# One gate over nine row tiles in place of two over four and five

## The chip, the core and the metric

The kernel runs on one core of one Trainium2 chip. The metric is the time on the device in microseconds (us), as the median of several executions; fewer is better. Six engines appear: TensorE (PE in the rows, with PEld for its weight loads), VectorE (DVE), ScalarE (ACT), GpSimd (POOL), SyncE (SP, which here only issues DMAs), and the DMA engines. Each of the first five works through its own queue of instructions strictly in order; an instruction whose input isn't there holds up everything behind it on that engine.

## The reference

Three stages follow one another on 2304 rows (4 sequences of 576) of 512 numbers.

```python
scores = scale * q @ k.T                       # 8 heads of 64, per sequence
thresh = max(scores) - tau
attn = softmax(where(scores >= thresh, scores, -1e9)) @ v      # x: 2304 x 512

noisy = x @ w_gate + log1p(exp(x @ w_noise)) * noise           # 8 experts
top2 = the two largest of noisy; weights = softmax over the two
out[row] = sum over its two experts of weight * relu(x @ w1[e]) @ w2[e]

# third stage: a skip score, the best of 8 experts, out = x + y for rows with a positive score
```

## The kernel before

**Attention.** Two heads are handled as a pair; four sequences of four pairs make 16 pairs (`PAIRS`). A pair is nine units of 128 rows of scores (`UNITS`), 144 in all. The loop over units (L770) is the schedule: it emits the scores of unit u+2 (`emit_S`, L291), the row maximum of u+1 (L299) and its exponential (L301), the transposes of the probabilities of u-1 (`emit_T`, L340, through one PSUM bank tagged `tp`) and the thresholded probabilities of u (L330). After a chunk of four or five units come products with v (`av`, L390 and L393) and the normalisation (`norm`, L400) into the transposed activations `xT`.

**Work in the background.** Between these steps the loop takes one step at a time from lists of generators: `bg` (gates), `bq` (first rows of expert 0), `fq` (fills and early weights), `pq` (scaling of k). `bg` is a queue: its second entry starts when the first has ended. A generator that yields 2 waits for a place where TensorE may be given work (`spare_pe`, L680, in six of the nine units of a pair); the others yield after about one VectorE instruction.

**The first gate.** `gate1(t0, n)` (L414) handles n row tiles of 128 rows: logits on TensorE in groups of up to four tiles (L157, transposed back at L162), some 45 small VectorE instructions on 128 x 8n elements, the rank of each row in its expert (`ranks`, L120: an array of n x 8 x n products and two matmuls, L135 and L136), the places of both choices (`ii`, L481), and then two scatters for each tile on POOL (L169) into the table `slots1`. Beside it `rows1` (L406) writes the n row tiles out to `x1` (L409 transposes, L411, L412). Logits, ranks, row transposes and the counts (`ct`, L630) all take the same PSUM bank as the transposes of the attention. `GATES` (L659) says at which pair and chunk the gates are put on `bg`: tiles 0 to 3 after pair 3, 4 to 8 after pair 7, 9 to 12 after pair 11; tiles 13 to 17 follow after the attention.

**The first experts.** Expert 0 starts on tiles 0 to 8 alone, expert 1 on tiles 0 to 12. `early_rows` (L711) is put on `bg` behind the second and the third gate. For expert 1 it loads `meta` from `slots1` by SP (L559), waits for all scatters so far, casts it to `tid` and `gid` on VectorE (L568, L570) and gathers rows of `x1` on POOL (L177). Then the layer of expert 0 begins: its weights are split in a high and a low part, `w1h` on ScalarE (L854) and `w1l` (L855) on POOL for the odd blocks and on VectorE for the even ones (L1135), and TensorE multiplies block by block (L612). The three first blocks are done earlier, in the last units (`early_mm1`).

Of the kernel before, what the change touches and what calls it, by code (L numbers as in the profile page):

```python
# [8 lines left out]
F32 = mybir.dt.float32  # L9
F32R = mybir.dt.float32r  # L10
I32 = mybir.dt.int32
# [11 lines left out]
E = 8  # L23
# [16 lines left out]
def attention_moe_moe(ctx, tc, qT, kT, vm, vr, tau, wgn, noise, w1a, w2a, wsg, w1b, w2b, out):  # L40
# [45 lines left out]
    wgn_t = const.tile([128, KD, 32], F32, name="wgn_t")  # L86
# [56 lines left out]
    def dot_e(pool, a, b, n, tag, r):  # L143
        w = pool.tile([128, n, E], F32, name="w" + tag)
        nc.vector.tensor_tensor(w, a, b, op=OP.mult)
        yield
        nc.vector.tensor_reduce(r[:, :, None], w, axis=AX.X, op=OP.add)
        yield

    def logits(pool, bank, parts, w, lz, i0):  # L150

        n = len(parts)
        yield 2
        ps = bank("lg")
# [48 lines left out]
    def pool(stack, name, bufs, side="left", **kw):  # L203
        return stack.enter_context(tc.tile_pool(name=name, bufs=bufs, side=side, reuse_waits="tile", **kw))
# [5 lines left out]
    g_p = pool(gctx, "g", 1)  # L210
# [7 lines left out]
    e_p = pool(actx, "e", 3, "right")  # L218
    pt_p = pool(actx, "pt", 2, "right")
    sm_p = pool(actx, "sm", 4, "right")  # L220
    ps_s = pool(actx, "ps_s", 3, space=PSUM)
    ps_x = pool(actx, "ps_x", 1, space=PSUM)
    ps_a = pool(actx, "ps_a", 1, space=PSUM)
# [9 lines left out]
    def xcols(t):  # L233
        return lambda kd: xTs[t * 128 // HN][:, kd, t * 128 % HN:t * 128 % HN + 128]
# [177 lines left out]
        nc.sync.dma_start(x1[t * 128:(t + 1) * 128, :], xr)  # L412

    def gate1(t0, n):  # L414
        sh = [128, n, E]
        lz = g_p.tile([128, n, 2 * E], F32, name="lz")
        for a in range(0, n, 4):
            yield from logits(g_p, bank, [xcols(t0 + i) for i in range(a, min(n, a + 4))], wgn_t, lz, a)
        z = lz[:, :, E:]
        u = g_p.tile(sh, F32, name="u")  # L420
        nc.vector.scalar_tensor_tensor(u, z, -1.0, z, op0=OP.mult, op1=OP.min)
        nc.scalar.activation(u, u, AF.Exp)
        yield from settle()
        w = g_p.tile(sh, F32, name="w")
        nc.vector.tensor_scalar(w, u, 2.0, None, op0=OP.add)
        yield
        nc.vector.reciprocal(w, w)
        yield
        nc.vector.tensor_tensor(w, w, u, op=OP.mult)
        yield  # L430
        nc.vector.tensor_tensor(u, w, w, op=OP.mult)
        yield
        ln = g_p.tile(sh, F32, name="ln")
        nc.vector.tensor_scalar(ln, u, 2.0 / 15, None, op0=OP.mult)
        yield
        for k in (13, 11, 9, 7, 5, 3):
            nc.vector.scalar_tensor_tensor(ln, ln, 2.0 / k, u, op0=OP.add, op1=OP.mult)
            yield
        nc.vector.scalar_tensor_tensor(ln, ln, 2.0, w, op0=OP.add, op1=OP.mult)
        yield  # L440
        nc.vector.scalar_tensor_tensor(ln, z, 0.0, ln, op0=OP.max, op1=OP.add)
        yield
        nz = g_p.tile(sh, F32, name="nz")
        nc.vector.tensor_tensor(nz, ln, noise_t[:, t0:t0 + n], op=OP.mult)
        yield
        nc.vector.tensor_tensor(nz, nz, lz[:, :, :E], op=OP.add)
        yield
        m1, o1 = yield from first_max(g_p, nz, n, "a")
        nc.vector.scalar_tensor_tensor(nz, o1, -3.0e38, nz, op0=OP.mult, op1=OP.add)
        yield  # L450
        m2, o2 = yield from first_max(g_p, nz, n, "b")
        mask = g_p.tile(sh, F32, name="mask")
        nc.vector.tensor_add(mask, o1, o2)
        d = g_p.tile([128, n], F32, name="d")
        nc.vector.tensor_sub(d, m2[:, :, 0], m1[:, :, 0])
        e2 = g_p.tile([128, n], F32, name="e2")
        nc.scalar.activation(e2, d, AF.Exp)
        yield
        rk = yield from ranks(g_p, bank, mask, run1, n)
        sl = g_p.tile(sh, F32, name="sl")  # L460
        nc.vector.tensor_tensor(sl, rk, ebase[:, None, :].to_broadcast(sh), op=OP.add)
        h7 = g_p.tile([128, n], F32, name="h7")
        nc.vector.tensor_scalar(h7, rk[:, :, E - 1], float(SL1), None, op0=OP.is_lt)
        yield
        dn = g_p.tile([128, n], F32, name="dn")
        nc.vector.tensor_scalar(dn, e2, 1.0, 1e-9, op0=OP.add, op1=OP.add)
        idx, meta = [], []
        for k in range(2):
            mt = g_p.tile([128, n, 2], F32, name=f"mt{k}")
            nc.vector.tensor_copy(mt[:, :, 0], tokid[:, t0:t0 + n])  # L470
            if k == 0:
                nc.vector.reciprocal(mt[:, :, 1], dn)
            else:
                nc.vector.tensor_tensor(mt[:, :, 1], e2, meta[0][:, :, 1], op=OP.mult)
            meta.append(mt)
            yield
        for k, o in enumerate((o1, o2)):
            ii = g_p.tile([128, n], I32, name=f"ii{k}")
            r = g_p.tile([128, n], F32, name=f"ir{k}")
            yield from dot_e(g_p, o, sl, n, "d", r)  # L480
            nc.vector.tensor_copy(ii, r)  # L481
            idx.append(ii)
            yield
        for i in range(n):
            for ii, mt in zip(idx, meta):
                scatter(slots1, ii[:, i:i + 1], mt[:, i], sc1)
                for _ in range(apart[0]):
                    yield 1
        nc.vector.tensor_tensor(h7, h7, mask[:, :, E - 1], op=OP.mult)
        nc.vector.tensor_scalar(not7[:, t0:t0 + n], h7, -1.0, 1.0, op0=OP.mult, op1=OP.add)  # L490
        yield
# [145 lines left out]
    bg = []  # L637
# [8 lines left out]
    def at(u, phase, f, *a):  # L646
        plan.setdefault((u, phase), []).append((f, a))
# [8 lines left out]
        return put  # L656

    WAITS = (4, 6)
    GATES = {(3, 1): (0, 4), (7, 1): (4, 5), (11, 1): (9, 4)}  # L659

    rq = []

# [107 lines left out]
    for u in range(NU):  # L770
        g, c, t, hh = UNITS[u]
        if (c, t, hh) == (0, 0, 0):
            if g + 1 < len(PAIRS):
                load_v(g + 1)
            if g == 12:
                early_pool()
                fq.append(early_raw())
                bq.append(early_xt())
            if g == len(PAIRS) - 1:
                pq.append(early_split())  # L780
        if (c, t, hh) == (0, 0, 0) and g + 2 < len(PAIRS):
            load_qk(g + 2)
        if (c, t, hh) == (1, 3, 0) and g + 2 < len(PAIRS):
            pq.append(prep(g + 2))
        if u + 2 < NU:
            emit_S(u + 2)
        else:
            early_mm1(u + 2 - NU)
        if u + 1 < NU:
            emit_max(u + 1)  # L790
        step(bg, 1, False)
        run(u, "mid")
        if u % 2 == 0:
            emit_th(u)
        step(bg, 1, False)
        step(bq, 1, False)
        if u:
            emit_T(u - 1)
        run(u, "pe")
        run(u, "end")  # L800
        emit_stt(u)
        step(pq)
        if u % 9 in (2, 3, 4, 6, 7, 8):
            spare_pe()
        else:
            step(bg, 1, False)
        if u % 4 == 3:
            step(fq)
        if (t, hh) == ((1, 1) if c == 0 else (4, 0)):
            k = (g, c)  # L810
            sums1(*k)
            at(u + 1, "mid", sums2, *k)
            at(u + 2, "pe", extra, *k)
            if c:
                at(u + 2, "pe", extra_mixed, g)
            for kt, (d, ph) in enumerate(AV[c]):
                at(u + d, ph, av, *k, kt)
            at(u + NORM[c][0], NORM[c][1], norm, *k)
            if k in GATES:
                at(u + 7, "end", bg.append, gate_and_rows(*GATES[k], True))  # L820
                if k[0] > 3:
                    at(u + 7, "end", bg.append, early_rows(*((e0a, 0) if k[0] == 7 else (e1a, 1))))
        if (c, t, hh) == (1, 2, 1):
            while pq:
                step(pq)
# [713 lines left out]
```

## Time and profile before

| | us |
|---|---|
| median of 3 runs | 1058.8 (1057.45 to 1059.7) |
| profiled execution | 1054.65 |
| its span, first to last instruction | 1052.9 |
| TensorE busy | 986.8 (94%) |
| VectorE busy | 586.3 (56%) |
| ScalarE busy | 495.0 (47%) |
| GpSimd busy | 305.9 (29%) |

The attention takes the first third: its last row maximum starts at 326.15. The rest is the two expert stages, in which TensorE is nearly always at work. Busy time of TensorE is that of matmuls which overlap, so 94% doesn't say that it could do no more. Where two engines hand work to and fro, the timeline shows who is late. "Clock" is the share of full speed that TensorE's clock was granted.

### The profile page before, as it was taken

Reading aid. Unit: us, or ns where it says so; the run is one execution under the profiler, and the core shown is the slowest. Engines: PE = TensorE matmul, PEld = TensorE weight load, DVE = VectorE, ACT = ScalarE, POOL = GpSimd, SP = SyncE. Lnnn points to the kernel's source line nnn. Section 1 sums busy time; section 2 is a strip of 40 time slices with the busy share of each in tenths; the row PEclk is TensorE's granted clock in tenths of the full one; section 3 lists DMA queues with packets and bytes.
Section 4 is the critical chain, followed back from the end, with each engine's and each line's share of the span. In section 5 each row is a group of like instructions: output and inputs, shape, how many; then the busy total and the mean of one; then the engine's idle time right before and its main releaser. Section 6 shows DMA issues by size and latency. Waiting matters only on the chain. (4 is left out here: it accounts for less than half of the span.)

```text
span 1052.9 us, 16933 instructions
## 1 busy us (share of the span) xinstructions
PE 986.8 (94%) x6262; PEld 776.4 (74%) x6262; DVE 586.3 (56%) x1480; ACT 495.0 (47%) x941; POOL 305.9 (29%) x417
## 2 busy tenths in 40 slices
PE   6999999999988898999999999999999987899995
PEld 3555555555545797889889998989898776799894
DVE  6887888787785762453333242423323365677463
ACT  4766766666665642343333333333333232555352
POOL 3121143126204542230313122121222366222210
PEclk9999999999999998999999999999999998899998
DMA  6434454145500654463535445252453730766550
GB/s 148 108 88 129 128 146 90 50 109 148 163 19 1 233 149 91 126 187 93 151 66 140 113 131 121 83 158 66 110 159 90 271 116 11 280 228 207 187 212 16
DMA packets 54856, 134.76 MB, mean 128 GB/s; under 512 B 20043, under 2 KB 26475, under 8 KB 46064
## 3 DMA queue, kind: packets, MB, share of 16 engines
q1 hardware_dynamic: 41344, 107.17, 32.7%
q0 software_dynamic: 13424, 26.45, 11.2%
q8 instruction: 51, 0.84, 0.4%
q14 instruction: 37, 0.30, 0.1%
HBM read 112.64 MB, written 23.69 MB: 129 GB/s over the span
## 5 line engine op out<-in xcount | busy, mean ns | idle before, releaser
L626 DVE SCALAR_TENSOR_TENSOR hl<-h,hh 128x128 fp32r<-128x128 f32 (+3 forms) x157 | 80.0, 510 | 166.3 <-ACT hh L625 147.1
L886 PE MATMUL y<-w2h,hh 128*128 128x512 f32 x418 | 170.4, 408 | 0.0
L886 PE MATMUL y<-w2h,hl 128*128 128x512 f32 x418 | 164.1, 393 | 0.0
L886 PE MATMUL y<-w2l,hh 128*128 128x512 f32 x418 | 163.4, 391 | 0.0
L625 ACT ACTIVATE hh<-h 128x128 fp32r<-128x128 f32 (+3 forms) x157 | 71.5, 455 | 193.5 <-PE h L612 147.4
L612 PE MATMUL h<-xh,w1h 128*128 128x320 f32 (+2 forms) x596 | 153.7, 310 | 2.7 <-ACT xh L594 1.4
L612 PE MATMUL h<-xh,w1l 128*128 128x320 f32 (+2 forms) x596 | 151.3, 306 | 2.1 <-POOL w1l L855 2.1
L612 PE MATMUL h<-xl,w1h 128*128 128x320 f32 (+2 forms) x596 | 151.9, 307 | 1.3 <-DVE xl L595 1.3
L299 DVE TENSOR_REDUCE nm<-s 128x1 f32<-128x576 f32 x144 | 108.6, 754 | 43.0 <-PE s L291 39.5
L291 PE MATMUL s<-kr,qr 64*128 64x288 f32 (+1 forms) x640 | 111.8, 458 | 9.2 <-DVE kr L274 5.4
L301 ACT ACTIVATE e<-s,nm 128x576 f32<-128x576 f32 x144 | 106.3, 738 | 20.6 <-DVE nm L299 13.3
L612 PEld LDWEIGHTS h<-xh,w1h 128*128 128x128 f32 x596 | 104.8, 190 | 4.7 <-ACT xh L594 1.9
L612 PEld LDWEIGHTS h<-xl,w1h 128*128 128x128 f32 x596 | 105.1, 190 | 2.5 <-DVE xl L595 2.4
L612 PEld LDWEIGHTS h<-xh,w1l 128*128 128x128 f32 x596 | 105.0, 190 | 2.3 <-POOL w1l L855 2.3
L330 DVE SCALAR_TENSOR_TENSOR P<-s,th,e 128x576 f32<-128x576 f32 x128 | 103.3, 807 | 3.8
L342 ACT ACTIVATE pt<-tp 128x512 f32<-128x512 f32 x128 | 76.4, 597 | 60.7 <-PE tp L340 53.4
L895 POOL DMA_INDIRECT out_dram<-yo,tid x35 | 56.1, 1602 | 168.0 <-ACT yo L894 90.7
L340 PEld LDWEIGHTS tp<-ident,P 128*128 128x128 f32 x512 | 54.3, 141 | 55.8 <-issue 13.9
L886 PEld LDWEIGHTS y<-w2h,hl 128*128 128x128 f32 x418 | 78.7, 188 | 17.6
L886 PEld LDWEIGHTS y<-w2h,hh 128*128 128x128 f32 x418 | 79.2, 189 | 14.5 <-issue 0.8
L886 PEld LDWEIGHTS y<-w2l,hh 128*128 128x128 f32 x418 | 79.1, 189 | 13.9
L340 PE MATMUL tp<-ident,P 128*128 128x128 f32 x512 | 84.7, 288 | 3.1 <-DVE xl L595 1.5
(270 smaller groups left out, 1455.0 us busy)
## 6 DMA issues: line engine op xcount, KB each, us to landing
rw<-in_w1a_dram SPq DMA_DIRECT2D x18, 1024.0 KB
rw<-in_w2a_dram SPq DMA_DIRECT2D x18, 1024.0 KB
qr<-in_qT_dram SPq DMA_DIRECT2D x30, 288.0 KB
rw<-in_w1b_dram SPq DMA_DIRECT2D x8, 1024.0 KB
rw<-in_w2b_dram SPq DMA_DIRECT2D x8, 1024.0 KB
kr<-in_kT_dram SPq DMA_DIRECT2D x96, 72.0 KB
out_dram<-zx SPq DMA_DIRECT2D x9, 512.0 KB
x<-xr SPq DMA_DIRECT2D x18, 256.0 KB
```

The lines of the kernel that those rows point to most:

```text
L291: nc.tensor.matmul(s[o, i, 0:SH], qr[r, h, t * 128:min((t + 1) * 128, S)], kr[r, h if t < 4 else 2 * h], start=True, stop=True)
L299: nc.vector.tensor_reduce(nm, s, axis=AX.XY, op=OP.max, negate=True)
L301: nc.scalar.activation(e, s, AF.Exp, bias=nm)
L330: nc.vector.scalar_tensor_tensor(o.rearrange("p (a b) -> p a b", a=2), s, th, e, op0=OP.is_ge, op1=OP.mult, accum_out=a)
L340: nc.tensor.transpose(ps[:, kt], P[:, c0 + kt * 128:c0 + (kt + 1) * 128], ident)
L342: nc.scalar.activation(ch["pt"][:, :, hh, (t % 2) * 128:(t % 2 + 1) * 128], ps, AF.Copy)
L612: nc.tensor.matmul(ps[:, c, 0:m], w[:, kd, :], v[:, kd, a:a + m], start=(kd == 0 and j == 0), stop=(kd == KD - 1 and j == 2))
L625: nc.scalar.activation(dh, src, AF.Relu)
L626: nc.vector.scalar_tensor_tensor(dl, src, 0.0, dh.bitcast(F32), op0=OP.max, op1=OP.subtract)
L886: nc.tensor.matmul(y, h[:, i * 128:(i + 1) * 128], w, start=(f == 0 and j == 0), stop=(f == KF - 1 and j == 2))
L895: nc.gpsimd.indirect_dma_start(out=x2[:, :], out_offset=bass.IndirectOffsetOnAxis(ap=tid, axis=0), in_=yo, in_offset=None, compute_op=OP.a ...
```

## The change

The gates at pair 3 (tiles 0 to 3) and pair 7 (tiles 4 to 8) become one at pair 7 over tiles 0 to 8. For a group of more than five tiles `gate1` takes its small tiles from a pool of its own, `g9_p`, in place of `g_p`. The third gate stays at pair 11 in the table, and `early_rows` is put behind both gates as before.

```diff
+    g9_p = pool(actx, "g9", 1, "right")
...
     def gate1(t0, n):
+        gp = g9_p if n > 5 else g_p
         sh = [128, n, E]
-        lz = g_p.tile([128, n, 2 * E], F32, name="lz")
+        lz = gp.tile([128, n, 2 * E], F32, name="lz")
...
-    GATES = {(3, 1): (0, 4), (7, 1): (4, 5), (11, 1): (9, 4)}
+    GATES = {(7, 1): (0, 9), (11, 1): (9, 4)}
...
                 at(u + 7, "end", bg.append, gate_and_rows(*GATES[k], True))
-                if k[0] > 3:
-                    at(u + 7, "end", bg.append, early_rows(*((e0a, 0) if k[0] == 7 else (e1a, 1))))
+                at(u + 7, "end", bg.append, early_rows(*((e0a, 0) if k[0] == 7 else (e1a, 1))))
```

The other lines of the diff put `gp` for `g_p` in the rest of `gate1`. The numbering of the lines moves by one or two. The change takes 49 of 1403 VectorE instructions out. What stands where it stood is counted in units: the ranks of the first two gates came after the transposes of units 60 and 101, and those of the joint gate come after 105; the logits of the third gate move from unit 116 to 125, its ranks from 134 to 143, the rows of expert 0 from 128 and 129 to 137 and 138.

TensorE at the ranks of the third gate, before (`s` scores, `tp` transposes of probabilities, `x` products with v, `Pm` the mixed unit of a pair):

```order
L291 MATMUL s<-kr,qr 128x288 x2
L340 MATMUL tp<-ident,P 128x128 x4
L393 MATMUL x<-rr,vz_174 128x256
L135 MATMUL rk<-mask,before 128x32
L136 MATMUL rk<-pre,ones 128x32
L291 MATMUL s<-kr,qr 128x288 x2
L340 MATMUL tp<-ident,Pm 128x128 x4
```

and now (`es` are weights of expert 0, which the last units multiply early):

```order
L614 MATMUL s<-xh,es 128x256
L341 MATMUL tp<-ident,P 128x128 x4
L394 MATMUL x<-rr,vz_177 128x256
L135 MATMUL rk<-mask,before 128x32
L136 MATMUL rk<-pre,ones 128x32
L341 MATMUL tp<-ident,Pm 128x128 x4
L614 MATMUL s<-xh,es 128x256
L614 MATMUL s<-xl,es 128x256
L614 MATMUL s<-xh,es 128x256 x2
```

The ranks stood among the scores of the last pair, and stand now between its last transposes.

POOL at the end of the attention, before (`slots` are the scatters, `xs` the gathers of expert 1's rows, `w1l` the splits of expert 0, `rb` and `Pm` work of the attention):

```order
L169 DMA slots_60<-mt_3790,ii_3821 18432x2
L168 MEMSET spacer 1x1
L169 DMA slots_60<-mt_3812,ii_3847 18432x2
L357 COPY rb<-sm 128x256
L359 COPY rb<-sm 128x128
L360 COPY Pm<-Pm 128x64
L177 DMA xs<-x_62,gid 128x512 x3
L855 TENSOR_TENSOR w1l<-rw_3097,w1h 128x512
L855 TENSOR_TENSOR w1l<-rw_3196,w1h 128x512 x2
```

and now:

```order
L169 DMA slots_60<-mt_3939,ii_3945 18432x2
L168 MEMSET spacer 1x1
L169 DMA slots_60<-mt_3942,ii_3952 18432x2
L177 DMA xs<-x_62,gid 128x512 x3
L856 TENSOR_TENSOR w1l<-rw_2988,w1h 128x512
L856 TENSOR_TENSOR w1l<-rw_3088,w1h 128x512 x2
```

All eight scatters stood ahead of the last attention work of POOL (`rb`, `Pm`), and now stand between it and the gathers; in both orders the splits come behind the gathers.

VectorE in the same place, before (`xT` is the normalisation, 128x320 the last one, `cntE` and `run` the counts):

```order
L400 TENSOR_TENSOR xT_172<-x,rr 128x256
L489 TENSOR_TENSOR h_3783<-h_3783,mask 128x4
L490 TENSOR_SCALAR not_117<-h_3783 128x4
L632 COPY cntE_4054<-ct 128x8
L741 TENSOR_SCALAR cntE_4054<-cntE_4054 128x8
L743 TENSOR_SCALAR cntE_4054<-cntE_4054,first_lane 128x8
L745 TENSOR_TENSOR run_113<-run_113,cntE_4054 128x1
L400 TENSOR_TENSOR xT_172<-x,rr 128x320
L568 CAST tid<-meta 128x3
L570 TENSOR_SCALAR gid<-meta 128x3
L855 TENSOR_TENSOR w1l<-rw_3196,w1h 128x512 x2
```

and now, from the second index cast on:

```order
L145 TENSOR_TENSOR wd<-fob,sl 128x32
L147 TENSOR_REDUCE ir_3953<-wd 128x4
L401 TENSOR_TENSOR xT_175<-x,rr 128x320
L483 CAST ii_3952<-ir_3953 128x4
L491 TENSOR_TENSOR h_3935<-h_3935,mask 128x4
L492 TENSOR_SCALAR not_117<-h_3935 128x4
L634 COPY cntE_3979<-ct 128x8
L743 TENSOR_SCALAR cntE_3979<-cntE_3979 128x8
L745 TENSOR_SCALAR cntE_3979<-cntE_3979,first_lane 128x8
L747 TENSOR_TENSOR run_113<-run_113,cntE_3979 128x1
L570 CAST tid<-meta 128x3
L572 TENSOR_SCALAR gid<-meta 128x3
```

Both casts `ii` (L483, L481 before) stood some thirty instructions ahead of the last normalisation; the second one is now behind it, and the instructions from `sl` on come after the normalisation before the last.

## Rows read from the trace of the kernel before

**Rows 1.** Busy time by pair of heads: us, engines (instructions), granted clock, DMA, GB/s

```profile
80.96:99.56 18.60, 18.25 (x123) 9.95 (x123) 15.28 (x37) 12.74 (x22) 4.16 (x7) 1.00 0.43 127
99.56:122.58 23.02, 22.17 (x172) 12.46 (x171) 17.14 (x53) 15.08 (x29) 4.16 (x7) 1.00 0.30 98
122.58:141.86 19.28, 18.94 (x127) 10.59 (x128) 17.10 (x58) 13.53 (x25) 4.16 (x7) 1.00 0.66 194
141.86:160.46 18.60, 18.25 (x123) 9.95 (x123) 16.63 (x54) 12.74 (x23) 11.58 (x22) 1.00 0.54 118
179.05:201.87 22.82, 22.07 (x173) 12.59 (x173) 16.04 (x42) 14.38 (x29) 4.16 (x7) 1.00 0.19 52
201.87:223.34 21.47, 20.77 (x138) 11.55 (x138) 18.06 (x64) 15.04 (x26) 4.17 (x7) 1.00 0.48 136
223.34:242.37 19.03, 18.66 (x127) 10.44 (x126) 17.25 (x59) 13.30 (x24) 5.34 (x10) 1.00 0.30 63
```

**Rows 2.** Timeline of POOL, end of attention: start, us, instruction [idle before, releaser]

```profile
331.27 0.96 POOL L169 DMA_INDIRECT slots<-mt,ii  x1 [0.22 <-issue]
...
343.41 1.20 POOL L177 DMA_INDIRECT xs<-x,gid  x1 [6.23 <-DVE gid L570]
...
347.15 3.73 POOL L855 TENSOR_TENSOR w1l<-rw,w1h 128x512 fp32r<-128x512 f32 x3
```

**Rows 3.** Timeline of SP and VectorE (DVE), same stretch

```profile
334.23 0.37 SPq L559 DMA_DIRECT2D meta<-slots  x1
...
337.00 0.41 DVE L400 TENSOR_TENSOR xT<-x,rr 128x256 f32<-128x256 f32 x1
...
342.50 0.49 DVE L400 TENSOR_TENSOR xT<-x,rr 128x320 f32<-128x320 f32 x1 [1.20 <-PE x L393]
...
342.90 0.16 DVE L568 CAST tid<-meta 128x3 int32<-128x3 f32 x1
```

**Rows 4.** Timeline of TensorE (PE), start of expert 0's layer

```profile
348.47 0.55 PE L612 MATMUL h<-xh,w1l 128*128 128x256 f32 x1 [2.14 <-POOL w1l L855]
```

**Rows 5.** Timeline of TensorE, ranks of the third gate and the next transposes

```profile
311.99 0.41 PE L135 MATMUL rk<-mask,before 128*128 128x32 f32 x2 [0.25 <-ACT pt L342]
...
313.24 0.66 PE L340 MATMUL tp<-ident,Pm 128*128 128x128 f32 x4
```

**Rows 6.** Timeline of TensorE, the count matmul and the products after it

```profile
340.04 0.39 PE L630 MATMUL ct<-run,ones 128*128 128x8 f32 x2
...
340.36 1.30 PE L390 MATMUL x<-pt,v 128*64 128x320 f32 x8
```

**Rows 7.** Timeline of VectorE, POOL and SP, the last gate

```profile
376.31 0.19 DVE L461 TENSOR_TENSOR sl<-rk,ebase 128x40 f32<-128x40 f32 x1
...
379.54 0.17 DVE L481 CAST ii<-ir 128x5 int32<-128x5 f32 x1
...
379.99 0.99 POOL L169 DMA_INDIRECT slots<-mt,ii  x1 [2.98 <-DVE ii L481]
...
391.17 0.96 POOL L169 DMA_INDIRECT slots<-mt,ii  x1 [0.21 <-issue]
...
392.44 0.96 POOL L169 DMA_INDIRECT slots<-mt,ii  x1 [0.23 <-issue]
...
395.47 0.38 SPq L559 DMA_DIRECT2D meta<-slots  x1
...
397.98 0.17 DVE L568 CAST tid<-meta 128x2 int32<-128x2 f32 x1 [4.26 <-DMA meta<-slots]
...
398.99 0.97 POOL L177 DMA_INDIRECT xs<-x,gid  x1 [5.59 <-DVE gid L570]
```

**Rows 8.** A later wait of TensorE, and stretches after two waits

```profile
402.41 1.11 PE L584 MATMUL xt<-ident,xs 128*128 128x128 f32 x4 [4.94 <-DMA xs<-x,gid]
...
348.47:351.45 2.98, 2.98 (x14) 2.98 (x15) 2.91 (x3) 0.47 (x2) 2.41 (x2) 0.51 0.77 245
...
402.41:405.60 3.19, 3.19 (x12) 2.79 (x13) 0.69 (x1) 0.60 (x1) 0.76 (x1) 0.50 0.73 129
```

More of the change, by code (lines that the diff above doesn't have):

```diff
@@ L414, in gate1 @@
     def gate1(t0, n):
+        gp = g9_p if n > 5 else g_p
         sh = [128, n, E]
-        lz = g_p.tile([128, n, 2 * E], F32, name="lz")
+        lz = gp.tile([128, n, 2 * E], F32, name="lz")
         for a in range(0, n, 4):
-            yield from logits(g_p, bank, [xcols(t0 + i) for i in range(a, min(n, a + 4))], wgn_t, lz, a)
+            yield from logits(gp, bank, [xcols(t0 + i) for i in range(a, min(n, a + 4))], wgn_t, lz, a)
         z = lz[:, :, E:]
-        u = g_p.tile(sh, F32, name="u")
+        u = gp.tile(sh, F32, name="u")
         nc.vector.scalar_tensor_tensor(u, z, -1.0, z, op0=OP.mult, op1=OP.min)
@@ L423, in gate1 @@
         yield from settle()
-        w = g_p.tile(sh, F32, name="w")
+        w = gp.tile(sh, F32, name="w")
         nc.vector.tensor_scalar(w, u, 2.0, None, op0=OP.add)
@@ L432, in gate1 @@
         yield
-        ln = g_p.tile(sh, F32, name="ln")
+        ln = gp.tile(sh, F32, name="ln")
         nc.vector.tensor_scalar(ln, u, 2.0 / 15, None, op0=OP.mult)
@@ L442, in gate1 @@
         yield
-        nz = g_p.tile(sh, F32, name="nz")
+        nz = gp.tile(sh, F32, name="nz")
         nc.vector.tensor_tensor(nz, ln, noise_t[:, t0:t0 + n], op=OP.mult)
@@ L447, in gate1 @@
         yield
-        m1, o1 = yield from first_max(g_p, nz, n, "a")
+        m1, o1 = yield from first_max(gp, nz, n, "a")
         nc.vector.scalar_tensor_tensor(nz, o1, -3.0e38, nz, op0=OP.mult, op1=OP.add)
         yield
-        m2, o2 = yield from first_max(g_p, nz, n, "b")
-        mask = g_p.tile(sh, F32, name="mask")
+        m2, o2 = yield from first_max(gp, nz, n, "b")
+        mask = gp.tile(sh, F32, name="mask")
         nc.vector.tensor_add(mask, o1, o2)
-        d = g_p.tile([128, n], F32, name="d")
+        d = gp.tile([128, n], F32, name="d")
         nc.vector.tensor_sub(d, m2[:, :, 0], m1[:, :, 0])
-        e2 = g_p.tile([128, n], F32, name="e2")
+        e2 = gp.tile([128, n], F32, name="e2")
         nc.scalar.activation(e2, d, AF.Exp)
         yield
-        rk = yield from ranks(g_p, bank, mask, run1, n)
-        sl = g_p.tile(sh, F32, name="sl")
+        rk = yield from ranks(gp, bank, mask, run1, n)
+        sl = gp.tile(sh, F32, name="sl")
         nc.vector.tensor_tensor(sl, rk, ebase[:, None, :].to_broadcast(sh), op=OP.add)
-        h7 = g_p.tile([128, n], F32, name="h7")
+        h7 = gp.tile([128, n], F32, name="h7")
         nc.vector.tensor_scalar(h7, rk[:, :, E - 1], float(SL1), None, op0=OP.is_lt)
         yield
-        dn = g_p.tile([128, n], F32, name="dn")
+        dn = gp.tile([128, n], F32, name="dn")
         nc.vector.tensor_scalar(dn, e2, 1.0, 1e-9, op0=OP.add, op1=OP.add)
@@ L468, in gate1 @@
         for k in range(2):
-            mt = g_p.tile([128, n, 2], F32, name=f"mt{k}")
+            mt = gp.tile([128, n, 2], F32, name=f"mt{k}")
             nc.vector.tensor_copy(mt[:, :, 0], tokid[:, t0:t0 + n])
@@ L477, in gate1 @@
         for k, o in enumerate((o1, o2)):
-            ii = g_p.tile([128, n], I32, name=f"ii{k}")
-            r = g_p.tile([128, n], F32, name=f"ir{k}")
-            yield from dot_e(g_p, o, sl, n, "d", r)
+            ii = gp.tile([128, n], I32, name=f"ii{k}")
+            r = gp.tile([128, n], F32, name=f"ir{k}")
+            yield from dot_e(gp, o, sl, n, "d", r)
             nc.vector.tensor_copy(ii, r)
```

## The prediction

> **What bounds the kernel now.** I read four views: busy time by stretch, one stretch for each pair of heads (to see what a gate costs the attention), the timeline at the end of attention (which engine is queued behind which), the waits of TensorE there, and the same steps at a later place, where the last gate runs through them.
>
> A pair of heads without a gate takes 18.60 us, first row of [rows 1]. With the first gate (tiles 0 to 3) the three pairs after it take 23.02, 19.28 and 18.60 us, so 5.10 us over 3 x 18.60; with the second (tiles 4 to 8) 22.82, 21.47 and 19.03, so 7.52 us over. What these rows have in common is not VectorE: the pair at 141.86 has 16.63 us of it busy against 15.28 and is exactly as long as a plain one. It is the single PSUM bank that the transposes of the attention (`tp`) share with logits, ranks and row transposes. The two gates use it 7 and 10 times (logits 2 and 4, rows 4 and 5, ranks 1 and 1): 12.62 / 17 = 0.74 us for a use.
>
> At the end of attention the third gate (tiles 9 to 12) feeds expert 1. Its last scatter starts on POOL at 331.27 and ends at 332.23, and the three gathers of expert 1's rows start at 343.41, first of them in [rows 2]; right behind them in POOL's queue stand the splits `w1l` of expert 0 at 347.15. [rows 3] shows why the gathers wait so long: the load of `meta` is issued at 334.23, 2.0 us after the last scatter, but VectorE casts it to `tid` only at 342.90, since `tid` stands behind the last normalisation (L400, 342.50) in its queue. So the scatters have slack today. TensorE itself waits 2.14 us at 348.47 for `w1l`, [rows 4]: it stands at the end of a chain through POOL that is already late. That chain is what the change touches.
>
> **The change part by part.**
>
> *Taken out:* one chain of gate arithmetic, 49 VectorE instructions, and one bank use. The nine tiles need logits in groups of four, four and one: 6 bank uses, with 9 for rows and 1 for ranks that is 16 in place of 17. Scatters stay 18. VectorE's share is hidden (the 141.86 row); the bank use is worth 0.74 us. Bounds: 0 if it falls where the bank is free, and 5.03 us if VectorE's work counts after all (the first gate adds 1.86, 1.82 and 1.35 us of it to its three pairs). I take 0.74, as it comes from a fit over both gates.
>
> *New tiles:* the large group has buffers of its own, so the third gate no longer waits for the scatters of the second to read theirs. Those landed long before; nothing.
>
> *Moved:* the background work is a queue. Nine tiles in one go end nine units (one pair of heads) later than 4 and 5 did, so the third gate's ranks come at the very end, and its index arithmetic and all eight scatters after the last row maximum. For the ranks in mid-attention that is another bank use less, 0.74 us: together 1.48 us earlier at the end of attention. From there I go in the clock of the trace before.
>
> 1. Ranks now stand ahead of the last transposes of a unit (`tp<-Pm`), on the same bank. From ranks to the next use of the bank took 1.25 us (311.99 to 313.24), [rows 5]. Everything after is 1.25 later. Bounds: 0 and 1.25; I take 1.25, because at the end of attention no other work fills the gap.
> 2. The count matmul `ct` leaves the place ahead of the last products: 340.36 - 340.04 = 0.32 us earlier, [rows 6]. The last normalisation goes from 342.50 to 342.50 + 1.25 - 0.32 = 343.43.
> 3. VectorE's order puts the second index cast (`ii` of the second choice) behind that normalisation; every second scatter needs it. What stands there now, `tid`, starts 0.40 after it [rows 3], so the cast starts at 343.83. The first choice's indices are no limit: from `sl` to its cast took 3.2 us in a busy stretch (376.31 to 379.54), [rows 7], and may start behind the normalisation before the last, at 337.00 + 0.41 + 1.25 = 338.66 [rows 3].
> 4. From the cast to its scatter 0.45 us (379.54 to 379.99) [rows 7]: the second scatter starts at 344.28. Six more at 1.27 us (391.17 to 392.44): the eighth starts at 351.90 and ends at 352.86 (0.96 each).
> 5. From the end of a last scatter to the first gather by way of `meta`, `tid` and `gid`: 393.40 to 398.99 = 5.59 us, [rows 7]. No earlier work hides it. The gathers start at 358.45 in place of 343.41.
> 6. Gathers to the first split 347.15 - 343.41 = 3.74 [rows 2], split to TensorE 348.47 - 347.15 = 1.32 [rows 4]: TensorE goes on at 363.51 in place of 348.47.
>
> That is 15.04 us. Three queues stand behind the one wait for `meta`: on SP the first two loads of expert 1's weights; on VectorE the casts, two splits of expert 0 and the last gate's chain; on POOL gathers and splits. TensorE waits for POOL's and has nothing else in order. Its wait grows from 2.14 to some 16 us, as TensorE itself arrives 0.93 later. Ends for steps 1 to 6: 13.8 (no delay by the ranks) and 15.1 (a longer slow clock). On the clock: in the 2.98 us after the wait of 2.14 us the granted clock is 0.51, the lower of its two levels (1.2 GHz); in the 3.19 us after a wait of 4.94 us it is 0.50, [rows 8]. Lost: 2.98 x 0.49 = 1.5 and 3.19 x 0.50 = 1.6 us. A wait twice as long costs 0.1 more, and today's is paid already; I leave it in the range.
>
> After that the layer of expert 0 is dense on TensorE and every later step (the last gate's arithmetic, loads released by splits) stands behind products of that layer, so the delay is carried along as it is.
>
> Sum: +15.04 - 1.48 = +13.6 us. The profiled execution took 1054.65 us (span 1052.90 and 1.75 around it): 1068.2. It lies 4.15 us under the median of the runs, 1058.8, to which I add the same: 1072.4 us.
>
> A rule that speaks for the change: the Trainium skill, "VectorE: DVE Perf Modes", section on the TRN2 errata, says that an instruction that reads SBUF pays a fixed latency however small it is, and that one large tile pays once where many small ones pay each time. By it, half the small instructions of two gates would be saved time. The trace has them as busy time, but the pair at 141.86 [rows 1] pays nothing for 1.35 us of them; by the rule the sum would be the second rival's.
>
> **The rivals.**
>
> - *The tail has slack enough (faster).* Today `meta` is ready some 6 us before it is used. If the eighth scatter ended by 343.41 - 5.59 = 337.82, nothing in the tail would move and the 1.48 us would be left: 1057.3. For it: `meta` is there by 334.23 + (397.98 - 395.47) = 336.74 [rows 3, 7] and used at 342.90. Against: seven scatters of 1.27 us behind a cast that waits for the last normalisation. It decides at that one instant, and I am 15 us past it. Not within 0.2% either (2.1 us, what a measurement here can tell from no change) unless the scatters end by about 341.
> - *VectorE's instructions are what the stage pays.* 5.03 us less in place of 0.74: -4.29, so 1068.1. Against: the 141.86 row. For: the 201.87 pair has most VectorE work, 18.06, and is 2.87 over.
> - *Given back later.* TensorE waits 4.94 us at 402.41 for rows that hang on the last gate's scatters, [rows 8]. If that gate's arithmetic runs on during the new wait, this is saved: 1067.5. Against: between its pieces stand VectorE instructions for products that TensorE hasn't made yet.
> - *More than rigid.* No gain in attention, the slow clock, and waits behind the stall that no row prices (I allow 1.8 us): 1072.4 + 1.48 + 0.1 + 1.8 = 1075.8.
> - *The change doesn't do what it says:* excluded, the order shows one group of nine.
>
> **How the numbers follow.** Forecast 0.62 (own range 1069 to 1075); given back 0.13; VectorE 0.08; more 0.08; slack 0.06; no change, by a mixture, 0.03. Low end: both partial gains together give 1072.4 - 4.94 - 4.29 = 1063.2, I stop at 1064; high end 1075.8 and the 1.1 us by which single runs of before differ from their median, 1077. Faster 0.06, same 0.03, slower 0.91.
>
> **What would show it.** Right: TensorE waits 15 to 18 us for `w1l` in one piece at the start of expert 0's layer; eight scatters in a row on POOL after the last normalisation, then a gap of 5 to 6 us, then three gathers, then the split; the stage before it 1 to 2 us shorter; the wait for gathered rows later on still 4 to 5 us. Wrong: no wait over 5 us there, scatters that end before the last normalisation, or an attention stage that is longer than before.

## The result and the profile after

The changed kernel takes 1071.4 us (median of four runs, 1068.6 to 1073.6) against 1058.1 us of the kernel before on the same chip (1057.3 to 1059.7): a ratio of 1.0129, 95% interval 1.0108 to 1.0151, so 13.3 us slower by the medians. The profiled execution took 1072.03 us; its span is 1070.2 us.

First the pairs of heads, as in [rows 1]: busy time by stretch, of the changed kernel, with the same columns (stretch, us, then busy time and instructions of PE, PEld, DVE, ACT and POOL, granted clock, DMA share, GB/s).

```profile
99.95:118.55 18.60, 18.26 (x123) 9.95 (x123) 15.49 (x38) 12.61 (x22) 4.15 (x7) 1.00 0.42 127
118.55:137.16 18.61, 18.27 (x123) 9.96 (x123) 15.19 (x38) 12.55 (x22) 4.15 (x7) 1.00 0.48 135
174.34:197.67 23.33, 22.58 (x201) 13.07 (x201) 15.67 (x38) 14.31 (x28) 4.14 (x7) 1.00 0.19 52
197.67:220.25 22.58, 21.73 (x144) 12.06 (x143) 17.75 (x52) 15.51 (x30) 4.15 (x7) 1.00 0.37 105
220.25:242.66 22.41, 21.37 (x139) 11.83 (x140) 19.43 (x58) 15.31 (x28) 4.16 (x7) 1.00 0.46 132
261.46:285.06 23.60, 21.07 (x135) 11.47 (x133) 15.83 (x45) 13.27 (x23) 15.78 (x28) 0.93 0.65 145
```

The two pairs that carried the first gate are plain now, 18.60 and 18.61 us where [rows 1] has 23.02 and 19.28. The three pairs with the gate of nine take 23.33, 22.58 and 22.41, which is 12.52 us over plain ones. The two gates before were 5.10 + 7.52 = 12.62 us over. So the joint gate saves 0.10 us, with 49 VectorE instructions fewer (1431 in this profile, 1480 before). The last row, the fourteenth pair, is longer than the 20.1 us that the same order of instructions takes in two experiments below. That comes back later.

Then the end of the attention, the timeline of VectorE, POOL and SP, which answers to [rows 2, 3]:

```profile
346.77 0.49 DVE L401 TENSOR_TENSOR xT<-x,rr 128x320 f32<-128x320 f32 x1 [4.72 <-PE x L394]
...
347.18 0.16 DVE L483 CAST ii<-ir 128x4 int32<-128x4 f32 x1
...
347.62 0.97 POOL L169 DMA_INDIRECT slots<-mt,ii  x1 [4.47 <-DVE not L492]
...
355.20 0.96 POOL L169 DMA_INDIRECT slots<-mt,ii  x1 [0.22 <-issue]
...
358.35 0.37 SPq L561 DMA_DIRECT2D meta<-slots  x1
...
360.20 0.17 DVE L570 CAST tid<-meta 128x3 int32<-128x3 f32 x1 [11.86 <-DMA meta<-slots]
...
361.20 1.22 POOL L177 DMA_INDIRECT xs<-x,gid  x1 [5.04 <-issue]
...
364.97 3.72 POOL L856 TENSOR_TENSOR w1l<-rw,w1h 128x512 fp32r<-128x512 f32 x3
```

The second index cast (`ii`) stands 0.41 us behind the last normalisation (L401), the second of the third gate's eight scatters 0.44 us behind the cast, and seven scatters run in a row to 356.16 (the first of the eight ran at 342.02, ahead of the normalisation). `meta` is loaded, cast to `tid` at 360.20, the three gathers follow and behind them the splits of expert 0. In [rows 2] the last scatter started at 331.27, well before the last normalisation. TensorE waits for the splits, as the timeline of TensorE shows; the second row is the later wait that [rows 8] has as 4.94 us:

```profile
366.30 0.58 PE L614 MATMUL h<-xh,w1l 128*128 128x256 f32 x1 [14.53 <-POOL w1l L856]
...
420.80 1.11 PE L586 MATMUL xt<-ident,xs 128*128 128x128 f32 x4 [5.41 <-DMA xs<-x,gid]
```

14.53 us in one piece, against 2.14 us at 348.47 in [rows 4]. The granted clock, by stretch, late in this wait and right behind it:

```profile
356.00:364.00 8.00, 0.00 (x0) 0.00 (x0) 2.43 (x8) 0.24 (x1) 2.35 (x4) 0.50 0.13 29
366.30:369.50 3.20, 3.20 (x15) 3.20 (x16) 0.25 (x1) 0.66 (x2) 2.39 (x2) 0.50 0.76 239
```

The clock is at its lower level (1.2 GHz, 0.50) while TensorE stands, and for at least 3.20 us more when it works again, about as long as after the short waits of [rows 8].

A second profile of each kernel, taken later on one chip, repeats this. The table has the start of the last normalisation, TensorE's first product with split weights of expert 0 (`w1l`), and the span of the profile, for these four and for the experiments. Each is read from the timeline of that run.

| kernel | last normalisation | first `w1l` product | between | span |
|---|---|---|---|---|
| before | 342.50 | 348.47 | 5.97 | 1052.9 |
| before, second profile | 342.96 | 348.94 | 5.98 | 1056.7 |
| changed | 346.77 | 366.30 | 19.53 | 1070.2 |
| changed, second profile | 344.60 | 363.98 | 19.38 | 1071.4 |
| e1, third gate late, old groups | 342.39 | 361.74 | 19.35 | 1064.8 |
| e2, gathers far behind splits | 341.68 | 352.42 | 10.74 | 1063.3 |
| e4, scatters of the joint gate close together | 350.76 | 360.08 | 9.32 | 1060.5 |
| e6, splits on VectorE | 341.82 | 356.87 | 15.05 | 1061.4 |
| e7, gathers right behind splits | 345.90 | 356.64 | 10.74 | 1062.9 |
| e3, before, gathers behind splits | 343.55 | 347.22 | 3.67 | 1054.2 |
| e9, e3 and splits on VectorE | 342.78 | 346.45 | 3.67 | 1049.8 |

From the last normalisation to TensorE's start the change adds 13.4 to 13.6 us. The last normalisation itself comes 1.6 to 4.3 us later. From the start on, 703.9 and 707.4 us are left against 704.4 and 707.8 before: nothing is given back.

### The profile page after: what moved, and what is told of

It is laid out like the page before. It is cut to its first block, busy times and chain, and to the rows that moved or that the text cites. A ratio compares the mean times of both kernels' runs of the same rounds, so it can differ in the third digit from the quotient of the medians.

```text
span 1070.2 us, 16869 instructions
## 1 busy us (share of the span) xinstructions
PE 989.2 (92%) x6258; PEld 776.5 (73%) x6258; DVE 580.5 (54%) x1431; ACT 493.7 (46%) x938; POOL 305.2 (29%) x417
## 5 line engine op out<-in xcount | busy, mean ns | idle before, releaser
L614 PE MATMUL h<-xh,w1l 128*128 128x320 f32 (+2 forms) x596 | 151.4, 307 | 14.5 <-POOL w1l L856 14.5
L614 PEld LDWEIGHTS h<-xh,w1l 128*128 128x128 f32 x596 | 105.0, 190 | 14.7 <-POOL w1l L856 14.7
L302 ACT ACTIVATE e<-s,nm 128x576 f32<-128x576 f32 x144 | 106.2, 737 | 20.4 <-DVE nm L300 14.5
L887 PEld LDWEIGHTS y<-w2h,hh 128*128 128x128 f32 x418 | 79.0, 189 | 14.5 <-issue 0.8
```

Source lines behind the costliest of these rows:

```text
L302: nc.scalar.activation(e, s, AF.Exp, bias=nm)
L614: nc.tensor.matmul(ps[:, c, 0:m], w[:, kd, :], v[:, kd, a:a + m], start=(kd == 0 and j == 0), stop=(kd == KD - 1 and j == 2))
L887: nc.tensor.matmul(y, h[:, i * 128:(i + 1) * 128], w, start=(f == 0 and j == 0), stop=(f == KF - 1 and j == 2))
```

## The experiments

The theory was that the loss is the chain on POOL behind the last normalisation: scatters, tokens' numbers, gathers, and only then the splits of expert 0. The rival was that the group of nine itself costs it. The experiments lie on three chips, and each was compared with the kernel before on its own chip: e1, e2, e4 and e6 on one (1051.9 us for the kernel before), c0, c1, e7 and e8 on a second (1058.4), f1, f2, e3 and e9 on a third (1059.5). So they are read by ratio. The changed kernel itself was run again on the second of these chips (c1), and not on the first.

**e1: the old groups, with the third gate late.**

```
-                at(u + 7, "end", bg.append, gate_and_rows(*GATES[k], True))
+                late = 10 if k[0] == 11 else 0
+                at(u + 7 + late, "end", bg.append, gate_and_rows(*GATES[k], True))
```

(and the same for `early_rows` of expert 1.)

> The kernel before, with its first two gates in groups of four and five as they were, and only the third gate (rows 9 to 12) put on the background list ten units later, so that its ranks come after the last unit and its second index cast stands behind the last normalisation, as in the changed kernel. Theory A (the loss is the chain on POOL behind the last normalisation: scatters, tokens' numbers, gathers, and only then the splits of the first expert's weights): about 13 us slower than before, near 1071, with a wait of TensorE for the split weights of 14 to 16 us at the start of the first expert. Rival B (the joint group of nine itself is the loss, by longer instructions on VectorE or by its pool): within 2 us of before, near 1058. Rival C (half and half): 1063 to 1066.

Measured: 1.0138 (1.0121 to 1.0155), +14.5 us. TensorE and VectorE, timeline of e1:

```profile
342.39 0.49 DVE L400 TENSOR_TENSOR xT<-x,rr 128x320 f32<-128x320 f32 x1 [3.01 <-PE x L393]
...
342.80 0.16 DVE L481 CAST ii<-ir 128x4 int32<-128x4 f32 x1
...
361.74 0.58 PE L612 MATMUL h<-xh,w1l 128*128 128x256 f32 x1 [15.36 <-POOL w1l L856]
```

The same cast behind the last normalisation and the same wait, 15.36 us, with groups of four and five. The group of nine isn't needed for the loss; the place of the third gate is. The rival falls. (About 13 us were expected.)

**e2: the gathers far behind the splits.** In the changed kernel, expert 1's `meta` is loaded where it was, and `load_ids` (casts and gathers) follows 18 steps later:

```
-            yield from early_ids(x, e)
+            load_early(x, e)
...
+    aux2.append(late_ids(e1a))      # 18 steps, then load_ids
```

> The changed kernel, the order of its gates untouched; only the second expert's token numbers and gathers are taken off their place and put behind POOL's splits of the first expert's weights. Theory A: the splits no longer stand behind the gathers, so TensorE's wait of 14.5 us nearly goes, and the time falls by about 14 us, to 1056 to 1058, if the gathered rows are still there in time for the second expert; up to 3 us of it is lost if they are not. Rival B (the loss lies in the attention or in the group of nine): it stays at 1069 to 1072.

Measured: 1.0131 (1.0112 to 1.0150), no gain that can be seen beside the 1.0129 and 1.0144 of the changed kernel, which was not run on this chip. The time alone is the rival's figure, so the waits have to decide. The timeline of e2, TensorE and POOL:

```profile
352.42 0.58 PE L614 MATMUL h<-xh,w1l 128*128 128x256 f32 x1 [6.74 <-POOL w1l L861]
...
368.53 0.98 POOL L177 DMA_INDIRECT xs<-x,gid  x1 [0.97 <-DVE ln L439]
...
373.48 1.09 PE L586 MATMUL xt<-ident,xs 128*128 128x128 f32 x4 [7.40 <-DMA xs<-x,gid]
```

The wait for splits fell from 14.5 to 6.74 us, as the theory had it. But the gathers now start at 368.53, and TensorE stands 7.40 us for their rows (`xs`) at expert 1, a wait that the changed kernel doesn't have. So the theory named the chain rightly, and I missed that its other end has a due time as well: most of what was gained at the splits (8.6 to 8.8 us from the last normalisation to the start) was lost at the gathered rows. I had allowed 3 us for that.

**e7: the gathers right behind the splits**, 5 steps in place of 18.

> The changed kernel with the second expert's token numbers and gathers directly behind POOL's three splits of the first expert's first weights (the run before had them some 14 us further on, and there TensorE's wait fell from 14.5 to 6.7 us and a wait of 7.4 us for the gathered rows took all of it back). Theory A: the wait for splits stays at 6 to 7 us, the wait for the gathered rows at the second expert goes, and the kernel is 5 to 7 us slower than before instead of 13 to 14. Rival: the gathers in front of the second weights' splits hold those up, a wait for these of 3 us or more appears, and 8 to 11 us remain. Rival B (it was never POOL's order): 12 us or more remain.

Measured: 1.0084 (1.0055 to 1.0112), 7.4 us slower by the medians, a little over the 5 to 7 expected. Timeline of e7:

```profile
355.31 3.73 POOL L861 TENSOR_TENSOR w1l<-rw,w1h 128x512 fp32r<-128x512 f32 x3
...
356.64 0.58 PE L614 MATMUL h<-xh,w1l 128*128 128x256 f32 x1 [4.46 <-issue]
...
361.23 1.01 POOL L177 DMA_INDIRECT xs<-x,gid  x1 [2.20 <-DVE gid L572]
...
412.44 0.66 PE L586 MATMUL xt<-ident,xs 128*128 128x128 f32 x4 [3.36 <-DMA xs<-x,gid]
```

TensorE starts 1.33 us after the first split, 10.74 us behind the last normalisation as in e2, and the wait at expert 1 is gone; the next one for gathered rows is the old one, 3.36 us at 412.44. That takes some 6 us from the loss of the changed kernel (1.0129 and 1.0144). What is left of the chain is 10.74 - 5.97 = 4.8 us, the scatters that still stand ahead of the splits, and 3 us by which the last normalisation is later than before.

**e6: all splits of expert 0's first weights on VectorE**, in the changed kernel.

```
-        w1split(e0a, f, nc.gpsimd if f % 2 else nc.vector)
+        w1split(e0a, f)
```

> The changed kernel with all splits of the first expert's first weights on VectorE, none on POOL. Theory A, with the scatters and the load of the tokens' numbers still in the chain and only the gathers and POOL's splits out of it: VectorE's queue holds the second half of the splits behind the cast of the tokens' numbers (360.20 in the changed kernel's profile), so TensorE starts the first expert some 4 to 5 us earlier, at about 361.5 instead of 366.3, and the time is about 1067. Rival (the gathers are not what holds the splits, they only stand beside them): no change, 1070 to 1072. Rival (VectorE's splits for the whole tile are slower than POOL's share): 1073 or more.

Measured: 1.0095 (1.0074 to 1.0117). Timeline of e6:

```profile
355.66 0.17 DVE L570 CAST tid<-meta 128x3 int32<-128x3 f32 x1 [12.26 <-DMA meta<-slots]
...
356.87 0.58 PE L614 MATMUL h<-xh,w1l 128*128 128x256 f32 x1 [11.06 <-DVE w1l L856]
```

TensorE waits for VectorE's splits, which stand behind the cast of `tid`: 15.05 us from the last normalisation where the changed kernel has 19.4 to 19.5. 4.4 us less, where 4 to 5 was expected.

**e8 and f1: both together.** e8 is e7 with the splits on VectorE; f1 moves the cast of `tid` one place further back in VectorE's queue (6 steps in place of 5).

> As the last one, and all splits of the first expert's first weights on VectorE, so that neither the eight scatters nor the gathers stand before them. Theory A: the wait for the splits falls to 0 to 2 us; the gathers, held by the scatters and the load of the tokens' numbers alone, come 1 to 2 us late for the second expert; the kernel is 1 to 3 us slower than before, which is what the attention stage and the gathers still cost. Rival (the tail of the attention lost more than that by the joint gate): 5 us slower or more.

> As the version with the gathers behind the splits and all splits on VectorE, with the cast of the tokens' numbers one place later in VectorE's queue, behind the first hidden tile's low part. There TensorE stood 5.5 us for that low part while VectorE waited for the load of the tokens' numbers. Theory: this wait falls to 0 to 2 us, 1 to 2 us come back at the second expert's gathered rows, and 1 to 3 us slower than before remain, the part that the attention stage costs. Rival (the next low part in VectorE's queue waits as long for the same load): 5 to 7 us slower, as there.

Measured: e8 1.0058 (1.0036 to 1.0079), f1 1.0079 (1.0055 to 1.0102). In e8 the first products with `w1l` come 5.36 us behind the last normalisation, but then (timeline of e8):

```profile
359.35 0.17 DVE L570 CAST tid<-meta 128x3 int32<-128x3 f32 x1 [6.77 <-DMA meta<-slots]
...
359.50 0.42 DVE L628 SCALAR_TENSOR_TENSOR hl<-h,hh 128x256 fp32r<-128x256 f32 x1
...
359.97 0.58 PE L614 MATMUL h<-xh,w1h 128*128 128x256 f32 x1 [5.50 <-DVE hl L628]
```

VectorE stands 6.77 us for `meta` in front of `tid`; the low part of the first hidden tile (`hl`) is queued behind it, and TensorE waits 5.50 us for that. In f1 one `hl` stands ahead of `tid`, and the next one waits (timeline of f1):

```profile
359.01 0.17 DVE L570 CAST tid<-meta 128x3 int32<-128x3 f32 x1 [3.58 <-DMA meta<-slots]
...
360.19 0.47 PE L614 MATMUL h<-xh,w1h 128*128 128x256 f32 x1 [2.58 <-DVE hl L628]
```

2.58 us in place of 5.50. The total doesn't tell e8 and f1 apart, and both stay 6 to 8 us slower than before, not the 1 to 3 I expected. The rivals named this time: in both places of the cast of `tid` in VectorE's queue, a low part that expert 0 needs is queued behind the wait for `meta`. The attention adds to it: in e8 the last normalisation is 2.9 us later than in c0 on the same chip.

**e4: less room between the joint gate's scatters**, so that the third gate comes earlier.

```
-                for _ in range(apart[0]):
+                for _ in range(1 if n > 5 else apart[0]):
```

> The changed kernel with one background step instead of several between the joint gate's scatters, so that the third gate's ranks come some five units earlier and three of its eight scatters are issued before the last attention work. Theory A: a dose in between; the last scatters end earlier by about 7 to 9 us, TensorE's wait for the split weights falls from 14.5 to 5 to 8 us, and the time comes to about 1064 (1062 to 1066). Rival B (the group itself): 1069 to 1072, as the changed kernel.

Measured: 1.0122 (1.0095 to 1.0148), the rival's figure and not the 1062 to 1066 of the theory. The wait for splits is 5.31 us, as expected, and 9.32 us after the last normalisation the layer starts. But that normalisation comes at 350.76, 9 us later than in e2 and e6 on the same chip. The timeline of e4 in the middle of the attention:

```profile
272.26 1.02 POOL L169 DMA_INDIRECT slots<-mt,ii  x1 [0.18 <-issue]
...
274.29 0.39 POOL L358 COPY rb<-sm 128x256 f32<-128x256 f32 x1
...
274.73 0.47 PE L370 MATMUL ex<-ident,rb 128*128 128x128 f32 x1 [4.85 <-POOL rb L358]
```

POOL's queue is full of scatters (0.96 to 1.02 us each) and of the scalings of k (1.01 to 1.02 us each), and the small copy `rb`, which the attention's own normalisation needs, comes late: TensorE stands 4.85 us for it. The fourteenth pair takes 29.81 us here:

```profile
261.54:291.35 29.81, 23.60 (x166) 13.25 (x166) 17.36 (x50) 14.05 (x27) 17.37 (x27) 0.83 0.43 97
```

That is 9.67 us more than in e6, with the wait and a lower clock (0.83) in it. The pair after it takes 26.24 us where e6 has 21.09, and from the start of the last pair to the last normalisation e4 takes 33.17 us and e6 38.95. Together these make the 9 us. Why the fifteenth pair is longer was not followed. So the dose was right at the end, and paid for in the middle.

**c0 and c1: second profiles of both kernels on one chip.**

> The kernel before, unchanged: a second profile of it, on the chip of this call. If the pieces of its attention stage repeat, the last row maximum comes at 326.15 us as in its first profile, within 0.5 us, and TensorE's wait for the first expert's split weights is again near 2.1 us. If pauses of some us in that stage come and go from run to run (the changed kernel's had one of about 3 us at 275 us, which two later runs with the same code at that place don't have), it may lie up to 4 us earlier or later.

> The changed kernel, unchanged, on the chip of this call, for a second profile. Theory: 1.011 to 1.015 times before, TensorE's wait for the split weights 14 to 16 us. The pair of heads with the pause at 275 us (23.60 us long) takes 20.1 us here if the pause was an accident of the run, 23.6 again if the change makes it.

Measured: c1 1.0144 (1.0121 to 1.0166). The last row maximum of c0 is at 326.47, that of c1 at 329.73 (330.22 in the first profile of the changed kernel). The wait for the splits is 2.14 us in c0 and 14.04 us in c1. The fourteenth pair of c1 is long again, 23.30 us, and the clock stays low longer after the wait than in the first profile:

```profile
261.27:284.57 23.30, 20.22 (x136) 10.98 (x135) 16.04 (x45) 13.16 (x23) 16.01 (x28) 1.00 0.65 147
363.98:369.00 5.02, 5.02 (x23) 5.02 (x24) 1.88 (x4) 1.45 (x3) 3.72 (x3) 0.50 0.88 305
```

**f2: the second load of w2a later.** In the changed kernel the fourteenth pair has a pause of some 3 us of TensorE, VectorE and ScalarE; e2 and e6, with the same order there, on another chip, don't have it (busy time by stretch, e6):

```profile
261.64:281.78 20.14, 19.80 (x136) 11.01 (x135) 15.96 (x45) 13.02 (x23) 15.96 (x28) 1.00 0.72 158
```

Just ahead of the pause a load of 1 MB has moved in SP's queue: it is issued at 266 in the changed kernel and at 285 before. f2 puts it behind the load of `meta` again:

```
         for k in range(4):
+            if k == 3:
+                yield
             rawload(e0a, k)
```

> The changed kernel with the second of the first expert's two loads of w2a (1 MB each) moved behind the load of the first early rows' meta in SP's queue. In the profiles before it goes out at 285 us, behind the residual rows; in those of the changed kernel at 266, directly behind the first. Theory (the 3 us pause at 275 us comes from the two loads beside the loads for the next pair): the fourteenth pair of heads takes 20.1 to 20.5 us instead of 23.3 to 23.6, the last row maximum comes at 326.5 to 327, and the kernel is 9 to 12 us slower than before instead of 13 to 15. Rival (the eighteen scatters of the joint gate or something else make the pause): 23 us and 13 to 15 us slower. On a chip where the changed kernel's order has no pause at all, as in three of the profiles above, the run tells nothing of it and shows 20.1.

Measured: 1.0112 (1.0089 to 1.0135), and the pair, with the load now at 281.70:

```profile
262.04:286.49 24.45, 21.53 (x136) 11.63 (x135) 16.04 (x45) 13.25 (x23) 16.08 (x28) 0.93 0.61 132
```

The pause stays, 24.45 us for the pair. This theory falls. What makes the pause is open: it shows in the first profile of the changed kernel and in all five with this order of the gates on two of the experiments' chips (23.3 to 24.9 us for the pair), and not in the two on the other (20.14 us each).

**e3 and e9: the same remedy in the kernel before.** e3 has the gathers behind POOL's three splits (5 steps), e9 in addition all these splits on VectorE.

> The kernel before, with the second expert's token numbers and gathers behind POOL's splits of the first expert's first weights; nothing of the gates changed. Theory: the 2.14 us that TensorE waits for POOL's splits there go, and the kernel is 1.5 to 2.5 us faster than before. Rival (what is saved comes back as a wait for the gathered rows at the second expert, or for the second weights' splits now behind the gathers): no difference, within 0.5 us.

> As the last one, and all splits of the first expert's first weights on VectorE. Theory: the same 1.5 to 2.5 us faster than before, not more, since TensorE's wait there is gone already; up to 3 us more if the three splits on POOL were still what it waited for. Rival: VectorE, with five splits of about 0.7 us instead of two in the last 10 us of the attention stage, holds up the last normalisation, and the kernel is 1 to 2 us slower than before.

Measured: e3 0.9974 (0.9959 to 0.9989), 2.5 us faster; e9 0.9924 (0.9908 to 0.9940), 1051.9 against 1059.5 us, 7.6 us faster. e9 is the one version that clearly beats both kernels. In neither is there a wait of 1 us or more for splits. The granted clock, by stretch, in e9:

```profile
348.00:356.00 8.00, 7.94 (x66) 7.64 (x65) 4.88 (x9) 5.98 (x13) 7.12 (x7) 1.00 0.88 312
```

1.00 where both profiles of the kernel before have 0.79 in these 8 us; e3 has 1.00 there too. TensorE is at the later wait for gathered rows at 398.93 (timeline of e9), in the kernel before at 402.41 and 402.44:

```profile
398.93 0.66 PE L584 MATMUL xt<-ident,xs 128*128 128x128 f32 x4 [4.10 <-DMA xs<-x,gid]
```

That is 3.5 us of the 7.6. Where the rest comes from is not shown, and there is no profile of the kernel before from that chip. Against e3, which is from the same chip (401.18 there), e9 is 2.25 us ahead at this wait and 4.4 us ahead at the end of the span. I had expected 1.5 to 2.5 us from the wait, and up to 3 more if POOL's splits still held TensorE; in e3 they don't, so the further gain has another cause, which stays open.

## Why the prediction was right

The time (1072.4 predicted, 1071.4 measured) and the main mechanism, the chain on POOL behind the last normalisation, hold. The term for the attention does not, and that the sum comes so near is partly luck. By its own steps:

- *Steps 3 and 4, cast and scatters:* 0.41, 0.44 and six times 1.26 us measured; 0.40, 0.45 and 1.27 predicted. Seven scatters stand behind the last normalisation, as these steps have it, and not the eight named as a sign. That these steps make the loss is shown by e1, which has them without the joint group and is as slow.
- *Step 5, from the last scatter's end to the gathers:* 361.20 - 356.16 = 5.04 us, predicted 5.59 from the last gate of the kernel before.
- *Step 6, gathers to splits to TensorE:* 3.77 and 1.33 us, predicted 3.74 and 1.32. That the splits wait because they stand behind the gathers in POOL's queue is shown by e2 and e7: 10.74 us from the last normalisation to TensorE's start in place of 19.4 to 19.5.
- *From the last normalisation to the start* all this was predicted as 363.51 - 343.43 = 20.08 us and is 19.53 and 19.38.
- *Step 1, ranks ahead of the transposes:* 0.92 us between the two, predicted 1.25; that they delay the last normalisation is not borne out, see below (timeline of TensorE in the changed kernel):

```profile
336.34 0.41 PE L135 MATMUL rk<-mask,before 128*128 128x32 f32 x2 [0.25 <-ACT pt L343]
...
337.26 0.66 PE L341 MATMUL tp<-ident,Pm 128*128 128x128 f32 x4 [0.29 <-ACT rk L138]
```

- *The attention, 1.48 us earlier:* this is the term that failed, and with it one of the prediction's signs of being wrong came: the attention is longer than before. The merging was to save one bank use, 0.74 us; it saves 0.10. The price of a use was all that two gates cost, divided by their bank uses, and the rows speak for another cost that I didn't consider, TensorE's own work. In the six pairs of [rows 1] that carry the gates TensorE is busy 11.4 us longer than in six plain ones, of 12.62 us; in the three pairs of the joint gate 10.9 us longer, of 12.52. Row transposes (5.9 us of busy time) and logits (3.2 us) are the same in both kernels. No run took the bank or this work away alone, so it isn't shown which of them a gate pays for.
- *The pause.* The last row maximum is 3.3 to 4.1 us later, mostly since the fourteenth pair has its pause of 3.2 to 3.5 us, which no step foresaw.
- *The third gate at the very end:* another 0.74 us less in mid-attention, and 1.25 - 0.32 = 0.93 us more behind it, so 0.19 us more in all. Busy time by stretch, from the end of the twelfth pair to the last normalisation (kernel before, c1, e2):

```profile
242.37:342.50 100.13, 91.03 (x638) 52.18 (x640) 72.00 (x224) 62.00 (x113) 35.14 (x64) 1.00 0.29 85
...
242.67:344.60 101.93, 91.11 (x631) 52.40 (x630) 73.62 (x228) 62.22 (x114) 37.55 (x69) 1.00 0.32 82
...
242.90:341.68 98.78, 90.69 (x631) 52.42 (x630) 73.54 (x228) 62.12 (x114) 37.54 (x69) 1.00 0.33 84
```

  Without the pause (e2, and e6 with the same 98.78) this takes 1.35 us less than before and 1.58 less than in c0 (100.36); in e1, with the old groups, it takes 98.90. c1 lies 3.15 us over e2, about the length of its pause. So the late place of the third gate seems to gain some 1.4 us where I had it cost 0.19, and the pause turns that into a loss. e1, e2 and e6 are of another chip than the profiles of the kernel before, but c1 without its pause comes to the same number.
- *The first profile of the changed kernel* loses 1.7 us more than c1 just ahead of the last normalisation, where its products run at a lower clock (first profile, then c1):

```profile
341.95:346.77 4.82, 4.82 (x20) 2.23 (x20) 0.10 (x2) 1.52 (x4) 1.12 (x2) 0.65 0.01 0
...
341.45:344.60 3.15, 3.15 (x20) 1.74 (x20) 0.10 (x2) 1.52 (x4) 1.13 (x2) 1.00 0.01 0
```

- *TensorE's wait of some 16 us:* 14.53 and 14.04, just under the 15 to 18 named as a sign. The pause doesn't explain that, since it moves both ends of the wait. The chain is some 0.6 us shorter, and TensorE begins to wait 5.00 and 5.34 us behind the last normalisation (19.53 - 14.53 and 19.38 - 14.04), where it was 3.83 (5.97 - 2.14) before; the prediction had carried the 3.83 over.
- *Carried along as it is:* shown, 703.9 and 707.4 us from the start to the end against 704.4 and 707.8. The rival of a gain given back fell with it: the later wait is 5.41 and 3.68 us against 4.94 and 4.04, and was not saved.
- *The rival of VectorE's instruction count* fell: 49 instructions less, and 0.10 us where it asked for 5.03. The rule of the Trainium skill behind it ("VectorE: DVE Perf Modes", section on the TRN2 errata) puts a fixed latency on each instruction of VectorE that reads SBUF, however small. That is VectorE's own time, and VectorE has time left in every one of these pairs: in the three with the joint gate it is busy for 15.67, 17.75 and 19.43 us of 23.33, 22.58 and 22.41.

So I had the last normalisation 0.55 us earlier than before (0.93 - 1.48), and it is 1.6 to 4.3 us later; the chain behind it I had 0.6 us too long. In the profiles that adds up to more than the 13.6 us of the forecast, 17.3 us between the first two spans and 14.7 between the second two. The medians are 13.3 us apart; the profiled run of the kernel before, 1054.65 us, lay below its other runs on that chip. The medians of the second pair (c1) are 15.0 us apart. So the first medians met the sum, and the other three differences are 1 to 4 us over it, by the pause and, in the first profile, by the slower products ahead of the last normalisation.

## What to carry to other kernels

When work on a background list is merged or moved, follow the last item of the list: what it releases, and which engine's queue that shares with the next stage's first work. A step that waits for a load (here the gathers, and the cast before them) belongs behind whatever the critical engine needs from the same queue, but no further: e2 lost at the gathered rows what it gained at the splits. A short wait in the old kernel, here 2.14 us, marks the place without slack; e3 took it out and won about its length, e9 won more, for a reason that isn't shown.

## What the runs showed of the hardware

- One large gate in place of two small ones saved 0.10 us of 12.62, though it has 49 VectorE instructions and one bank use less; TensorE's busy time for it fell from 11.4 to 10.9 us.
- Most scatters take POOL 0.95 to 1.04 us each (two in the first profile of the changed kernel 1.19 and 1.29) and start 1.26 us apart when they stand in a row; TensorE stood 4.85 us for a copy of 0.39 us that came behind scatters and scalings (e4).
- The pause of some 3 us in the fourteenth pair, in six profiles of eight with this order of the gates, isn't explained. It isn't the second load of w2a (f2).
- After a wait of 14 us TensorE stays at its lower clock for at least 3.2 us in one profile and at least 5.0 us in another of the same kernel; after waits of 2 and 5 us it was about 3 us ([rows 8]).
